# A recurrence and a token mixer on one core: v permuted on TensorE for every unit, uncentred decays, one-piece X sums and another order of steps

## Chip, core and metric

The kernel runs on one core of one Trainium2 chip, in one launch. The metric is device time in microseconds (us). The engines are TensorE (PE, with its weight loads as PEld), VectorE (DVE), ScalarE (ACT), GpSimd (POOL) and SyncE (SP), which issues nearly all DMAs.

## The reference, cut to what matters

Inputs r, k, v, w have shape (4 batches, 8 heads, 768 tokens, 48), u is (8, 48). A recurrence gives x of 384 columns per token, and a mixer over all tokens of a batch follows.

```python
for t in range(S):
    cur = np.einsum('bhd,bhe->bhde', u[None] * kt, vt)
    y[:, :, t] = np.einsum('bhd,bhde->bhe', rt, state + cur)
    state = wt[:, :, :, None] * state + np.einsum('bhd,bhe->bhde', kt, vt)
x = y.transpose(0, 2, 1, 3).reshape(B, S, H * D)
W_tok = scale * (x @ w_q) @ (x @ w_k).T          # per batch, 768 x 768
out = np.maximum(W_tok @ x, 0.0) @ w_out
```

## The kernel before, in words

Each batch's 768 tokens are three **units** of 256 tokens, so there are 12 units, 0 to 11; a unit is two chunks of 128 tokens. `unit(n, batch)` declares the steps of a unit, each with the engines that may do it:

- Loads by SP into rings of four buffers: `wg`, `kg`, `rg`, `vg`. `load` brings rows of two tokens of a head (96 values, 384 bytes), `load_long` rows of four tokens (768 bytes). In the last batch (units 9 to 11) v comes instead as `vw`: four loads for the whole batch, each of runs of one token (48 values, 192 bytes).
- `ln` (ACT) takes the log of the decays into `lw`; `cw` (PE) sums them along the tokens; `ep` and `en` (ACT) are the exponentials of plus and minus those sums. The log is offset by a constant MU, which centres the sums; `gx`, `gv`, `gk`, the scaled mask `US` and the scaled identity `IDU` undo that later.
- `k16`, `r16`, `v16` are casts to bf16. `kT`, `rT` (PE) transpose k and r with the permutation `PM`; `vp` (PE) permutes v's tokens in four products of 64x384, and `VB` copies the result out of PSUM. In the last batch `VB` is cast by POOL straight from `vw`, with no `v16` and no `vp`.
- `ks` copies kT; `qT`, `RT`, `KT` are products of r and k with each other and with the exponentials. `A` (PE) is KT by RT for each head, and `AM` (DVE) multiplies it with the causal mask US. `kb`, `kd` turn KT back; `sn` (PE) and `SB` (DVE) are the running state. `uT` and `UB` transpose u once, and `dps`, `dd`, `Vd` make the bonus of a token's own value.
- `yi` and `ya` (PE) sum state and mask products, and `X` (DVE) adds `Vd`: X = y * gx + Vd, in two instructions of 384 columns.
- `xt`, `XT`, `qk`, `QK` (in the last unit `wq`, `wk` and their copies) make the mixer's queries and keys from X. After a batch's last unit, `T` sums keys by X over the batch and `TS` copies it; then for each unit `mx` (PE), `rl` (relu), `fp` (PE, six products with w_out for a whole step, three for a half one), `os` (copy) and `st` (store). In the first and last unit several steps come in halves.

The order is a table: `ORDER` lists the step numbers, `WAYS` gives the engine (or form) of each step that has a choice, `BANKS` the PSUM bank of each buffer. In `WAYS`, A, D, P are ScalarE, VectorE, GpSimd; E, e, c are forms of products; d is a KT product read from PSUM. Every engine runs its own steps in that order and waits for what each needs. Eighteen products of zeros warm TensorE up at the start, and twelve more (`z`) stand in the table. The functions that the change touches:

Of the kernel before, what the change touches and what calls it, by code (L numbers as in the profile page):

```python
# [32 lines left out]
class Plan:  # L33
# [89 lines left out]
]  # L123
WAYS = (
    "PDDDAPPDDdPADPPDDEEEAAPPAdPAAPEAcEEAAPPAPPADPeDEEDAAAAAAAAPPDPDADPeAcEEDAPPAdPAAPEAEEEDA"
    "PPDPPAAPeAEEAAAAAAAAAAPDPPAAPEDEcEAAPPDPPDAPEAEEEAAPPDPPAAPeDceAAAAADADDPAAPPAPEDcEEDAPP"
    "DPPAPeAcceAAPPDPPPAPPAEEDDAEDADAAADAAAADADDA"
)
BANKS = [
# [13 lines left out]
def kernel(  # L143
# [12 lines left out]
    nc = tc.nc  # L156
# [15 lines left out]
    WHOLE = (B - 1,)  # L172

    SHIFT = 25
    MU = -SHIFT * math.log(2.0) / C
    UNIT = 2.0 ** -SHIFT

# [9 lines left out]
    def const(shape, dtype, name):  # L187
# [15 lines left out]
        QK=(2, QW, BF16), TS=(2, DM, BF16), vw=(2, NCH * DM, F32))  # L203
    if not WHOLE:
        del RINGS["vw"]
# [15 lines left out]
    IDU = const([C, C], BF16, "IDU")  # L221
    Z = const([C, 512], BF16, "Z")
    US = const([C, C], F32, "US")
    CM = const([C, 2 * C], BF16, "CM")
    pos0 = const([C, 1], I32, "pos0")
    pos1 = const([C, 1], I32, "pos1")
    gx = const([C, 1], F32, "gx")
    gv = const([C, 1], F32, "gv")
    gk = const([C, 1], F32, "gk")
# [18 lines left out]
    def setup():  # L248
# [9 lines left out]
        for q in range(4):  # L258
            rows = ds(64 * (q % 2) + 32 * (q // 2), 32)
            nc.gpsimd.iota(pos0[rows, :], pattern=[[0, 1]], base=q, channel_multiplier=4)  # L260
            nc.gpsimd.iota(pos1[rows, :], pattern=[[0, 1]], base=q + 1, channel_multiplier=4)
# [632 lines left out]
```

## Time and profile before

| | |
|---|---|
| median of 3 runs | 101.71 us (101.36 to 102.08) |
| span of the profiled execution, first to last instruction | 99.6 us (the only time given of that execution) |
| busy, share of the span | PE 87%, DVE 85%, ACT 79%, POOL 70% |
| DMA, mean | 24.68 MB in 45141 packets, 248 GB/s |
| granted TensorE clock | full throughout |

Busy times are unions of an engine's instructions; matmuls are pipelined and their ends are modelled, so a busy PE is not PE at its peak. In a timeline row stand start, duration, engine, source line, operation and output <- inputs with their shapes, and in brackets the idle time ahead and what ended it. Instructions of one engine overlap a little, so the distance from one start to the next is what a step costs its queue. A group row has busy time, mean duration of one in ns, and idle time ahead.

### The profile page before, as it was taken

How to read it: one execution, taken by the hardware profiler on the slowest of the kernel's cores; microseconds unless marked ns; L12 is line 12 of the kernel's file. 1: busy time of each engine (PE TensorE's matmuls, PEld its weight loads, DVE VectorE, ACT ScalarE, POOL GpSimd, SP SyncE). 2: the span in 40 equal slices, each digit the busy share in tenths (PEclk: the TensorE clock that was granted, in tenths of full speed). 3: DMA queues.
4: the chain of work that ended last, by engine and by line, in shares of the span. 5: the costliest groups of instructions: out<-in, count | busy, mean ns of one | idle time of the engine just before them, and what ended most of it. 6: DMA issues, size and time to landing. Idle time of an engine off the chain costs nothing.

```text
span 99.6 us, 4492 instructions
## 1 busy us (share of the span) xinstructions
PE 86.6 (87%) x1906; PEld 63.3 (64%) x1911; DVE 84.9 (85%) x154; ACT 79.0 (79%) x135; POOL 69.5 (70%) x82
## 2 busy tenths in 40 slices
PE   5978796879886998999999999889998999999930
PEld 1325473756774767777776777759787687776610
DVE  6284999799979999979999999999999799783740
ACT  6034998799996799899999998999899766666920
POOL 6866354999799895799999989498996392500000
PEclk9999999999999999999999999999999999999999
DMA  1999999799999999999999977998993056030794
GB/s 17 313 327 349 324 337 296 195 295 335 289 314 298 225 311 329 344 321 268 271 330 305 316 114 218 251 156 201 282 417 115 7 210 264 10 158 7 277 367 149
DMA packets 45141, 24.68 MB, mean 248 GB/s; under 512 B 31552, under 2 KB 43968, under 8 KB 45120
## 3 DMA queue, kind: packets, MB, share of 16 engines
q1 hardware_dynamic: 44960, 24.19, 84.0%
q8 instruction: 15, 0.25, 0.9%
q10 hardware_dynamic: 160, 0.20, 0.5%
q14 instruction: 6, 0.05, 0.1%
HBM read 19.66 MB, written 4.72 MB: 245 GB/s over the span
## 4 chain that ended last, share of the span: by engine, by line
PE 37%; DVE 23%; SPq 20%; DMA 7%; issue 7%; ACT 3%; ACTq 0%; DVEq 0%
PE PS L179 37%; SPq L232 9%; SPq L237 8%; DMA vg<-in_v_dram 7%; DVE AM L595 7%; DVE X L710 6%; DVE RT L516 3%; SPq L355 2%; DVE qT L506 2%; DVE ks L333 2%; DVE SB L658 1%; ACT VB L327 1%; SPq L357 1%; ACT MX L339 1%; DVE kd L335 1%
## 5 line engine op out<-in xcount | busy, mean ns | idle before, releaser
L595 DVE TENSOR_TENSOR AM<-PS,US 128x1024 bf16<-128x1024 f32 x24 | 28.8, 1218 | 0.7 <-PE PS L179 0.7
L526 POOL TENSOR_TENSOR KT<-ks,en 128x1024 bf16<-128x1024 bf16 (+1 forms) x10 | 19.7, 1965 | 4.7 <-DVE ks L333 3.3
L575 POOL TENSOR_TENSOR Vd<-VB,dd 128x768 bf16<-128x768 bf16 (+1 forms) x14 | 18.1, 1293 | 4.5 <-ACT dd L327 3.4
L454 ACT ACTIVATE en<-PS 128x1024 bf16<-128x1024 f32 (+1 forms) x14 | 12.5, 907 | 3.0 <-PE PS L179 2.9
L179 PEld LDWEIGHTS <-KT 48*128 48x128 bf16 (+1 forms) x312 | 9.7, 94 | 6.6 <-issue 4.5
L447 ACT ACTIVATE ep<-PS 128x512 bf16<-128x512 f32 (+1 forms) x28 | 13.7, 555 | 0.1
L179 PE MATMUL PS<-wo,MX 128*128 128x384 bf16 x72 | 13.5, 327 | 0.0
L710 DVE SCALAR_TENSOR_TENSOR X<-PS,gx,Vd 128x384 bf16<-128x384 f32 x22 | 12.5, 609 | 0.7 <-PE PS L179 0.6
L407 ACT ACTIVATE lw<-wg 128x768 bf16<-128x768 f32 x12 | 10.3, 857 | 2.9 <-DMA wg<-in_w_dram 2.9
L179 PE MATMUL PS<-RT,KT 48*128 48x128 bf16 x192 | 9.7, 218 | 1.2 <-ACT VB L327 0.4
L327 ACT COPY os<-PS 128x768 f32<-128x768 f32 (+1 forms) x11 | 7.9, 714 | 3.5 <-PE PS L179 3.5
L418 POOL CAST k<-kg 128x768 bf16<-128x768 f32 x10 | 8.3, 827 | 2.5 <-DMA kg<-in_k_dram 2.5
L179 PE MATMUL PS<-Z 128*128 128x512 bf16 x25 | 8.4, 461 | 1.4 <-DVE Z L250 1.2
L418 POOL CAST r<-rg 128x768 bf16<-128x768 f32 x10 | 8.2, 825 | 1.6 <-DMA rg<-in_r_dram 1.6
L179 PEld LDWEIGHTS <-MX 128*128 128x128 bf16 x72 | 6.5, 97 | 3.6 <-DVE MX L341 0.2
L516 DVE TENSOR_TENSOR RT<-PS,ep 128x1024 bf16<-128x1024 bf16 (+1 forms) x14 | 8.4, 605 | 0.0
L179 PE MATMUL PS<-VB,AM 128*128 128x48 bf16 x192 | 8.0, 184 | 0.4 <-issue 0.4
L506 DVE TENSOR_TENSOR qT<-PS,ks 128x1024 bf16<-128x1024 bf16 x12 | 8.2, 684 | 0.1
L339 ACT ACTIVATE MX<-PS 128x768 bf16<-128x768 f32 (+1 forms) x12 | 8.0, 682 | 0.4
L179 PE MATMUL PS<-CM,lw 64*128 64x128 bf16 x192 | 7.4, 217 | 0.5 <-DVE AM L595 0.3
L327 ACT CAST VB<-PS 128x768 bf16<-128x768 f32 x8 | 6.4, 804 | 1.1 <-PE PS L179 0.6
L179 PEld LDWEIGHTS <-AM 128*128 128x128 bf16 x192 | 6.3, 96 | 1.6 <-issue 0.7
(90 smaller groups left out, 191.9 us busy)
## 6 DMA issues: line engine op xcount, KB each, us to landing
kg<-in_k_dram SPq DMA_DIRECT2D x12, 384.0 KB, 6.4
wg<-in_w_dram SPq DMA_DIRECT2D x12, 384.0 KB, 5.0
rg<-in_r_dram SPq DMA_DIRECT2D x12, 384.0 KB, 5.8
vg<-in_v_dram SPq DMA_DIRECT2D x9, 384.0 KB, 6.3
out_dram<-os SPq DMA_DIRECT2D x9, 384.0 KB, 2.5
vw<-in_v_dram SPq DMA_DIRECT2D x4, 288.0 KB, 6.7
out_dram<-os SPq DMA_DIRECT2D x5, 192.0 KB, 2.4
wof<-in_moe_w_out_dram SPq DMA_DIRECT2D x1, 576.0 KB, 6.2
```

Source lines behind the costliest of these rows:

```text
L179: return nc.tensor.matmul(o, l, rr, start=start, stop=stop, skip_group_check=True, is_transpose=trans)
L327: nc.scalar.copy(o, i)
L407: nc.scalar.activation(view(lw.tile, 0, [[64, H], [512, 2], [1, D]]), view(g["wg"].tile, 0, [[D2, H], [D, 2], [1, D]]), ACT.Ln, bias=0.0, ...
L418: op(view(o.tile, 0, [[64, NP], [256, 4], [1, D]]), view(g[src].tile, 0, [[2 * D2, NP], [D, 4], [1, D]]))
L447: nc.scalar.activation(view(ep.tile, cs[0] * NP * EW + off, [[EW, NP * len(cs)], [step, 2], [1, 32]]), view(at(cw), cs[0] * 512 + j * 64, ...
L454: nc.scalar.activation(en.tile[:, ds(cs[0] * 512, w_)], at(cw)[:, ds(cs[0] * 512, w_)], ACT.Exp, bias=0.0, scale=-1.0)
L506: lambda e: nc.vector.tensor_tensor(plain(qT.tile), turned(512), plain(ks.tile), ALU.mult),
L516: nc.vector.tensor_tensor(plain(RT.tile, cs, 32), turned(512, cs, True), plain(ep.tile, cs, EW // 4), ALU.mult)
L526: x.tensor_tensor(KT.tile[:, cols], ks.tile[:, cols], en.tile[:, cols], ALU.mult)
L575: (nc.vector if e == "D" else nc.gpsimd).tensor_tensor(Vd.tile[:, cols], VB.tile[:, cols], view(dd.tile, cs[0] * H, [[1, len(cs) * H], [0, ...
L595: AMs[c] = add(("AM", n, c), "D", lambda e, c=c, A=A: nc.vector.tensor_tensor(view(AM[c].tile, 0, [[C, 8], [1, C]]), view(at(A), 0, [[C, 8 ...
L710: nc.vector.scalar_tensor_tensor(view(X.tile, 2 * i * DM + hh * D, [[D2, H], [1, D]]), view(at(y), hh * 512, [[D, H], [1, D]]), gx, view(V ...
```

## The change

1. Units 1 to 11 load v with `load_long`, in rows of four tokens. `v16` holds it in another layout, and `vp` has 16 products (8 groups of 32 output rows and 192 columns for each half of the heads) instead of four. `vw` and `load_whole` are gone, so units 9 to 11 have `v16`, `vp` and `VB` like the others. Unit 0 keeps its four products.
2. The decays are not centred: `ln` has scale 1, and the position fills, `gx`, `gv`, `gk`, `IDU` and the scaling of US are gone. `kd` is a plain copy, and `sn` uses the plain identity.
3. X is one sum of y and Vd over 768 columns, and in the last unit two of 384.
4. `ORDER`, `WAYS` and `BANKS` are new tables throughout.

```diff
-    WHOLE = (B - 1,)
-    SHIFT = 25
-    MU = -SHIFT * math.log(2.0) / C
-    UNIT = 2.0 ** -SHIFT
...
-        nc.scalar.activation(gx, pos0, ACT.Exp, bias=0.0, scale=MU)
-        nc.scalar.activation(gv, pos1, ACT.Exp, bias=0.0, scale=-MU)
...
-        nc.vector.tensor_scalar_mul(IDU, ID16, UNIT)
-        nc.vector.tensor_scalar_mul(gk, gv, UNIT)
-        nc.vector.tensor_scalar_mul(US, US, gv)
...
-        for name, ap in (("wg", w), ("kg", k), ("rg", r)) + (() if whole else (("vg", v),)):
-            f = load_long if name in ("kg", "rg") and long else load
+        for name, ap in (("wg", w), ("kg", k), ("rg", r), ("vg", v)):
+            f = load_long if name != "wg" and long else load
...
-                                 bias=0.0, scale=math.exp(-MU))
+                                 bias=0.0, scale=1.0)
...
-        if whole:
-            VBs = add(("VB", n), "PAD", lambda e: copy(
-                e, view(VB.tile, 0, [[D, H], [DM, 2], [1, D]]),
-                view(batch["vw"].tile, 2 * i * D, [[NCH * D, H], [D, 2], [1, D]])),
-                batch["vwL"], VB, [batch["vw"]], cols=2 * DM)
+        v16, vp = ring("v16"), wide()
+        if long:
+            v16v, vgv = [[D, NP], [NP * D, 4], [1, D]], [[2 * D2, NP], [D, 4], [1, D]]
         else:
...
+            if long:
+                for hq in range(2):
+                    for s in range(4):
+                        for c in range(2):
+                            mm(x[ds((s % 2) * 64 + (s // 2) * 32, 32),
+                                 ds(c * 512 + hq * NP * D, NP * D)],
+                               PM[ds(c * 64, 64), ds(c * 64 + hq * 32, 32)],
+                               v16.tile[ds(c * 64, 64), ds(s * NP * D, NP * D)])
+                return
...
-                copy(e, view(kd.tile, 64 + cs[0] * 1024, [[256, n4], [128, 2], [1, D]]), x, gk)
+                copy(e, view(kd.tile, 64 + cs[0] * 1024, [[256, n4], [128, 2], [1, D]]), x)
...
-                    mm(x[rows, ds(0, NP * D)], IDU[:, rows], old.tile, start=True, stop=False)
+                    mm(x[rows, ds(0, NP * D)], ID16[:, rows], old.tile, start=True, stop=False)
...
-                for hh in range(2) if not end else ():
-                    nc.vector.scalar_tensor_tensor(
-                        view(X.tile, 2 * i * DM + hh * D, [[D2, H], [1, D]]),
-                        view(at(y), hh * 512, [[D, H], [1, D]]), gx,
-                        view(Vd.tile, hh * D, [[D2, H], [1, D]]), ALU.mult, ALU.add)
+                if not end:
+                    nc.vector.tensor_tensor(
+                        view(X.tile, 2 * i * DM, [[D, 2], [D2, H], [1, D]]),
+                        view(at(y), 0, [[512, 2], [D, H], [1, D]]),
+                        view(Vd.tile, 0, [[D, 2], [D2, H], [1, D]]), ALU.add)
...
 ORDER = [
-    0, 3, 13, 2, 21, 22, 23, 15, 16, 17, 1, 24, 25, 26, 27, 28, 29, 76, 77, 78, 31, 73, 74, 75,
+    0, 1, 2, 3, 4, 15, 16, 17, 30, 21, 22, 23, 24, 25, 26, 33, 34, 36, 27, 28, 29, 31, 14, 18,
```

What the tables move is seen in the engines' queues, of which three places follow. A name like `ks_0_95` is buffer 0 of the ring `ks`; `PS_62` is PSUM.

**VectorE at the start**, from the cast of u to the first mask product of unit 0; ahead of it stand the setup's fills, before also the scaling of US and the pads of both `kd` buffers, after the pads of one. Before:

```order
L333 CAST uC_134<-uR_133 8x128
L333 COPY ks_0_95<-PS_62 128x1024
L526 TENSOR_TENSOR KT_0_101<-ks_0_95,en_0_93 128x512
L521 TENSOR_TENSOR KT_0_101<-PS_62,en_0_93 128x512
L516 TENSOR_TENSOR RT_0_99<-PS_62,ep_0_91 128x512
L506 TENSOR_TENSOR qT_0_97<-PS_62,ks_0_95 128x1024
L335 TENSOR_SCALAR kd_0_83<-PS_62,gk_152 128x8x48
L516 TENSOR_TENSOR RT_0_99<-PS_62,ep_0_91 128x512
L335 TENSOR_SCALAR kd_0_83<-PS_62,gk_152 128x8x48
L595 TENSOR_TENSOR AM0_0_111<-PS_62,US_146 128x1024
```

After:

```order
L300 CAST uC_132<-uR_131 8x128
L382 CAST r16_0_87<-rg_0_67 128x8x2x48
L300 COPY UB_133<-PS_62 128x8
L300 COPY ks_0_95<-PS_62 128x1024
L467 TENSOR_TENSOR qT_0_97<-PS_62,ks_0_95 128x1024
L482 TENSOR_TENSOR KT_0_101<-PS_62,en_0_93 128x512
L477 TENSOR_TENSOR RT_0_99<-PS_62,ep_0_91 128x512
L482 TENSOR_TENSOR KT_0_101<-PS_62,en_0_93 128x512
L477 TENSOR_TENSOR RT_0_99<-PS_62,ep_0_91 128x512
L562 TENSOR_TENSOR AM0_0_111<-PS_62,US_143 128x1024
```

The cast of r and the copy of UB have come in ahead of ks, and the two kd copies have gone to ScalarE. On TensorE, `uT`, `kT` and `cw` of unit 0 stood in that sequence, and now `cw`, `kT`, `rT`, `uT`; on SP, `wg` is now loaded ahead of `kg`.

**VectorE from ks of unit 10 to a mask product of unit 9.** Before:

```order
L333 COPY ks_0_95<-PS_62 128x1024
L710 SCALAR_TENSOR_TENSOR X_0_125<-PS_62,gx_150,Vd_0_109 128x8x48 x2
L506 TENSOR_TENSOR qT_0_97<-PS_62,ks_0_95 128x1024
L516 TENSOR_TENSOR RT_0_99<-PS_62,ep_0_91 128x1024
L335 TENSOR_SCALAR kd_1_84<-PS_62,gk_152 128x16x48
L595 TENSOR_TENSOR AM0_1_112<-PS_62,US_146 128x1024
L658 TENSOR_TENSOR SB_3_118<-PS_62,ep_1_92 128x192
L595 TENSOR_TENSOR AM1_1_114<-PS_62,US_146 128x1024
```

After:

```order
L300 COPY ks_0_95<-PS_62 128x1024
L300 COPY XT_1_120<-PS_62 128x768
L467 TENSOR_TENSOR qT_0_97<-PS_62,ks_0_95 128x1024
L677 TENSOR_TENSOR X_0_125<-PS_62,Vd_0_109 128x2x8x48
L477 TENSOR_TENSOR RT_0_99<-PS_62,ep_0_91 128x1024
L300 COPY kd_1_84<-PS_62 128x16x48
L300 COPY XT_0_119<-PS_62 128x768
L562 TENSOR_TENSOR AM0_1_112<-PS_62,US_143 128x1024
L625 TENSOR_TENSOR SB_3_118<-PS_62,ep_1_92 128x192
L300 CAST QK_0_127<-PS_62 128x384
L562 TENSOR_TENSOR AM1_1_114<-PS_62,US_143 128x1024
```

Two XT copies and a QK copy, which were ScalarE's, stand here now; X is one instruction.

**GpSimd in units 9 to 11.** Before, from KT of unit 9 on:

```order
L526 TENSOR_TENSOR KT_1_102<-ks_1_96,en_1_94 128x1024
L526 TENSOR_TENSOR KT_0_101<-ks_0_95,en_0_93 128x1024
L333 CAST VB_1_106<-vw_0_131 128x8x2x48
L333 CAST VB_0_105<-vw_0_131 128x8x2x48
L575 TENSOR_TENSOR Vd_1_110<-VB_1_106,dd_1_108 128x768
L418 CAST k16_1_90<-kg_3_74 128x4x4x48
```

After, from KT of unit 10 on:

```order
L487 TENSOR_TENSOR KT_0_101<-ks_0_95,en_0_93 128x1024
L300 CAST v16_0_103<-vg_2_77 128x4x4x48
L542 TENSOR_TENSOR Vd_1_110<-VB_1_106,dd_1_108 128x768
L300 CAST v16_1_104<-vg_3_78 128x4x4x48
L379 CAST k16_1_90<-kg_3_74 128x4x4x48
```

Where GpSimd wrote VB of units 9 and 10 itself, it now casts v of units 10 and 11 into v16, and TensorE (`vp`) and ScalarE (`VB`) finish them; on TensorE both those `vp` stand ahead of `ya` of unit 9. On SP the last loads were `vw` (three), `kg`, `wg`, `rg`, then all stores; now they are `vg` (unit 9), `wg`, the store of unit 1, `vg` (10), `vg` (11), `kg`, `rg`, then the other stores.

More of the change, by code (lines that the diff above doesn't have):

```diff
@@ L202 @@
         SB=(4, NP * D, BF16), XT=(2, 2 * DM, BF16), MX=(4, 2 * DM, BF16), X=(2, NCH * DM, BF16),
-        QK=(2, QW, BF16), TS=(2, DM, BF16), vw=(2, NCH * DM, F32))
-    if not WHOLE:
-        del RINGS["vw"]
+        QK=(2, QW, BF16), TS=(2, DM, BF16))
     tiles = {k: [const([C, w_], ty, f"{k}_{i}") for i in range(n)]
@@ L322, in at, with copy @@
         return x if dtype == F32 else x.bitcast(dtype)
-    def copy(e, o, i, by=None):
+    def copy(e, o, i):
         if e == "A":
-            if by is None:
-                nc.scalar.copy(o, i)
-            else:
-                nc.scalar.activation(o, i, ACT.Copy, bias=0.0, scale=by)
-        else:
-            x = nc.gpsimd if e == "P" else nc.vector
-            if by is None:
-                x.tensor_copy(o, i)
-            else:
-                x.tensor_scalar_mul(o, i, by)
+            nc.scalar.copy(o, i)
+        else:
+            (nc.gpsimd if e == "P" else nc.vector).tensor_copy(o, i)
     def relu(e, o, i):
@@ L388, in unit @@
         fine = each if split else both
-        whole, long = b in WHOLE, n in LONG
+        long = n in LONG
         g = {}
-        for name, ap in (("wg", w), ("kg", k), ("rg", r)) + (() if whole else (("vg", v),)):
-            f = load_long if name in ("kg", "rg") and long else load
+        for name, ap in (("wg", w), ("kg", k), ("rg", r), ("vg", v)):
+            f = load_long if name != "wg" and long else load
             g[name] = ring(name)
@@ L398, in unit @@
                 bonus(g["wgL"])
-        if whole and i == 0:
-            batch["vw"] = ring("vw")
-            batch["vwL"] = [dma(("vw", n, q), lambda e, q=q, x=batch["vw"].tile:
-                                load_whole(b, q, x), buf=batch["vw"]) for q in range(4)]
         lw = ring("lw")
@@ L535, in unit @@
         VB = ring("VB")
-        if whole:
-            VBs = add(("VB", n), "PAD", lambda e: copy(
-                e, view(VB.tile, 0, [[D, H], [DM, 2], [1, D]]),
-                view(batch["vw"].tile, 2 * i * D, [[NCH * D, H], [D, 2], [1, D]])),
-                batch["vwL"], VB, [batch["vw"]], cols=2 * DM)
-        else:
-            v16, vp = ring("v16"), wide()
-            v16s = add(("v16", n), "PAD", lambda e: copy(
-                e, view(v16.tile, 0, [[D, H], [DM, 2], [1, D]]),
-                view(g["vg"].tile, 0, [[D2, H], [D, 2], [1, D]])), [g["vgL"]], v16, [g["vg"]])
-            def f_vp(e):
-                x = at(vp)
-                for j in range(2):
-                    for c in range(2):
-                        rows = ds(c * 64, 64)
-                        mm(x[ds(j * 64, 64), ds(c * 512, DM)], PM[rows, rows],
-                           v16.tile[rows, ds(j * DM, DM)])
-            vps = add(("vp", n), "E", f_vp, [v16s], vp, [v16], mode=3)
-            VBs = add(("VB", n), "AD", lambda e: copy(
-                e, view(VB.tile, 0, [[DM, 2], [1, DM]]), view(at(vp), 0, [[512, 2], [1, DM]])),
-                [vps], VB, [vp], cols=2 * DM)
+        v16, vp = ring("v16"), wide()
@@ new lines, in unit, with f_vp @@
+        if long:
+            v16v, vgv = [[D, NP], [NP * D, 4], [1, D]], [[2 * D2, NP], [D, 4], [1, D]]
+        else:
+            v16v, vgv = [[D, H], [DM, 2], [1, D]], [[D2, H], [D, 2], [1, D]]
+        v16s = add(("v16", n), "PAD", lambda e: copy(
+            e, view(v16.tile, 0, v16v), view(g["vg"].tile, 0, vgv)), [g["vgL"]], v16, [g["vg"]])
+        def f_vp(e):
+            x = at(vp)
+            if long:
[7 more added lines that the diff above has]
+                return
+            for j in range(2):
+                for c in range(2):
+                    rows = ds(c * 64, 64)
+                    mm(x[ds(j * 64, 64), ds(c * 512, DM)], PM[rows, rows],
+                       v16.tile[rows, ds(j * DM, DM)])
@@ L559, in unit @@
+        vps = add(("vp", n), "E", f_vp, [v16s], vp, [v16], mode=4 if long else 3)
+        VBs = add(("VB", n), "AD", lambda e: copy(
+            e, view(VB.tile, 0, [[DM, 2], [1, DM]]), view(at(vp), 0, [[512, 2], [1, DM]])),
+            [vps], VB, [vp], cols=2 * DM)
         dps, dd = bank(), ring("dd")
```

29 lines of the change are left out of this document (7 added, 22 removed), and 90 rows, old and new, of tables (BANKS, ORDER).

## Prediction

> **What bounds the kernel now.** I read the engine totals first, then the table by stretch, then the chain that ended last, and last each engine's timeline.
>
> ```profile
> PE 86.6 (87%) x1906; PEld 63.3 (64%) x1911; DVE 84.9 (85%) x154; ACT 79.0 (79%) x135; POOL 69.5 (70%) x82
> ...
> 40.00:50.00 10.00, 9.64 (x234) 7.44 (x232) 9.45 (x16) 9.62 (x16) 9.55 (x8) 1.00 1.07 301
> 60.00:70.00 10.00, 9.42 (x276) 7.47 (x274) 10.00 (x17) 9.64 (x16) 8.24 (x7) 1.00 1.00 214
> 80.00:90.00 10.00, 9.84 (x189) 7.48 (x190) 8.84 (x17) 6.07 (x13) 4.14 (x4) 1.00 0.41 160
> ```
>
> In the rows by stretch the pairs of figures are PE, PEld, DVE, ACT, POOL, then the granted clock, the DMA share and GB/s. From 40 to 70 us VectorE (DVE) has no slack worth the name, ScalarE (ACT) little, and the DMA engines are full. From 80 us on only TensorE is full. The chain names the same change of hands.
>
> ```profile
> 65.98 1.14 DVE AM L595
> ...
> 67.17 9.67 PE PS L179 x260
> ...
> 85.56 10.02 PE PS L179 x107
> ```
>
> So the time is: VectorE's queue up to its last mask product `AM` (85.57 us), and then some 14 us of small steps that no queue shortens much: the last X, its products, the last batch's token products and output projections, the store. I therefore sum what the change does to VectorE's queue up to that product, then ask what the others allow.
>
> **Durations on VectorE**, as distance from one start to the next, since neighbours overlap by some 0.08 us:
>
> ```profile
> 28.62 1.31 DVE L333 CAST v<-vg 128x768 bf16<-128x768 f32 x1 [0.73 <-DMA vg<-in_v_dram]
> 29.85 0.68 DVE L506 TENSOR_TENSOR qT<-PS,ks 128x1024 bf16<-128x1024 bf16 x1
> ...
> 31.05 1.13 DVE L710 SCALAR_TENSOR_TENSOR X<-PS,gx,Vd 128x384 bf16<-128x384 f32 x2
> 32.10 0.67 DVE L521 TENSOR_TENSOR KT<-PS,en 128x1024 bf16<-128x1024 bf16 x1
> 32.70 0.16 DVE L333 COPY dd<-PS 128x16 f32<-128x16 f32 x1
> 32.85 0.56 DVE L333 COPY XT<-PS 128x768 bf16<-128x768 bf16 x1
> 33.38 1.23 DVE L595 TENSOR_TENSOR AM<-PS,US 128x1024 bf16<-128x1024 f32 x1
> 34.52 0.35 DVE L658 TENSOR_TENSOR SB<-PS,ep 128x192 bf16<-128x192 f32 x1
> ...
> 54.19 0.61 DVE L335 TENSOR_SCALAR kd<-PS,gk 128x768 bf16<-128x768 bf16 x1
> 54.71 1.22 DVE L595 TENSOR_TENSOR AM<-PS,US 128x1024 bf16<-128x1024 f32 x1
> ...
> 56.11 0.95 DVE L333 CAST VB<-PS 128x768 bf16<-128x768 f32 x1
> 56.97 0.68 DVE L333 COPY ks<-PS 128x1024 bf16<-128x1024 bf16 x1
> ```
>
> *X.* A unit's X is now two instructions, 32.10-31.05 = 1.05 us. It becomes one sum of 768 columns, which the trace does not show. From below, AM does 1024 fp32 columns from PSUM in 34.52-33.38 = 1.14 us, so 768 of them 0.855; from above, nothing is gained (1.05). The VB copy of 768 fp32 columns took 56.97-56.11 = 0.86, and I take 0.87: 0.18 us for each of 11 units, **-2.0 us**; the ends are 0 and -2.2.
>
> *Steps that the new order hands out differently*, counted up to the last AM. Off VectorE: the cast of v of unit 3 (29.85-28.62 = 1.23), the VB copy of unit 7 (0.86), two `dd` copies (0.15 each), and of `kd` six calls become three. The six were two of 768 columns (0.52) and four of 384 (some 0.33 by 54.71-54.19 less the 0.2 us that half the columns save), 2.35 in all; three of 768 make 1.55. Together -3.2 us. Onto VectorE: three XT copies (33.38-32.85 = 0.53), two QK copies of 384 fp32 columns (about half of VB's, 0.45), one ks (its 0.68 less the overlap, 0.6), and `KT`: two whole units of 32.70-32.10 = 0.60 both now and after, two half calls now and four after, 0.6 us more for the two. Together +3.7 us. The sum is **+0.5 us**, and with X **-1.5 us** on VectorE.
>
> *Start.* What precedes the first AM moves most.
>
> ```profile
> 1.23 5.73 PE L179 MATMUL PS<-Z 128*128 128x512 bf16 x18 [1.23 <-DVE Z L250]
> 7.64 0.17 PE L179 MATMUL PS<-ID,uC 8*128 8x8 bf16 x1 [0.68 <-DVE uC L333]
> ...
> 6.69 0.83 POOL L421 CAST r<-rg 128x768 bf16<-128x768 f32 x1 [0.73 <-DMA rg<-in_r_dram]
> ...
> 8.52 0.69 DVE L333 COPY ks<-PS 128x1024 bf16<-128x1024 bf16 x1 [0.94 <-PE PS L179]
> ...
> 12.62 1.22 DVE L595 TENSOR_TENSOR AM<-PS,US 128x1024 bf16<-128x1024 f32 x1
> ```
>
> The warm-up products leave TensorE at 1.23+5.73 = 6.96 us, but it then waits until 7.64 for `uC`, which VectorE casts behind the scaling of US and two sets of pads; the transpose of k and the decay sums stand behind that. In the changed order the decay sums come first, then kT and rT, and only then uC's transpose, so TensorE can begin at about 7.0, and ScalarE's exponentials follow. Against that, VectorE now casts r of unit 0 (1.23 us as for v, from 6.69, when rg has landed) and waits for uC's transpose behind rT, so ks starts at about 8.6, as now. From there to AM it has qT, two KT and two RT, 0.6 + 0.6 + 4 x 0.33 = 2.5 us, where 12.62-8.52 = 4.1 us passed: AM at about 11.2, 1.4 us sooner. Some 0.65 of it are the two `kd` calls counted above. **-0.7 us**, between 0 and -1.4. The scaling of US, the scaled identity, GpSimd's eight position fills and two exponentials, which the change drops, all lie ahead of that first ks, so they have no other price.
>
> *End.* After the product T of the last unit TensorE now has five whole projections of six products; the changed order has four (one whole, six halves), and the fifth stands where the last XT is copied.
>
> ```profile
> 83.96 1.14 PE L179 MATMUL PS<-wo,MX 128*128 128x384 bf16 x6
> ```
>
> TensorE waits little there now, so a projection mostly moves: I give it **-0.3 us**, between 0 and -1.1, its own length.
>
> *TensorE.* v goes through 16 products of 32x192 output where there were 4 of 64x384, and the three units of the last batch, which had none, get them too.
>
> ```profile
> 37.05 0.36 PE L179 MATMUL PS<-v,PM 64*64 64x384 bf16 x4
> 37.34 0.40 PE L179 MATMUL PS<-RT,KT 48*128 48x128 bf16 x8
> ...
> 50.15 0.40 PE L179 MATMUL PS<-PM,r 64*128 64x64 bf16 x16
> 50.48 0.35 PE L179 MATMUL PS<-UB,qT 128*128 128x2 bf16 x8
> ...
> L179 PE MATMUL PS<-v,PM 64*64 64x384 bf16 x36 | 3.2, 346 | 0.7 <-DVE RT L516 0.7
> ```
>
> Four products of 346 ns each fit into 0.36 us, so those on different quarters of the array run side by side; the step occupies 37.34-37.05 = 0.29 us. The new ones use eighths, so two rounds of eight of half the length. Below: the same 0.29; above, if sixteen cost as sixteen transposes do plus the columns, 50.48-50.15 = 0.33 for 64 columns, three times that for 192, 1.0 us. Nearest is the row of the same data, and I take 0.40: 8 x 0.11 + 3 x 0.40 = 2.1 us more. Beside VectorE's queue most of it is hidden; between 67 and 77 us, where the chain runs through TensorE, 1.2 us come together, and I charge **+0.8 us** in all.
>
> The Trainium skill speaks against these sixteen: "TensorE: Matmul & The Clock Gate", The mechanism, has weight loads overlap running products only where their row group differs, and eight of the sixteen share each row group. By that rule the sum would be the last rival's below. The trace does not agree: products three and four of the step at 37.05 share row groups with the first two, and all four are done within 0.36 us.
>
> *ScalarE* gets four more VB copies in all and gives up XT, QK and ks, and `kd` loses its scale, 901 ns against 800 for an XT of the same size:
>
> ```profile
> L329 ACT ACTIVATE kd<-PS,gk 128x768 bf16<-128x768 bf16 x5 | 4.5, 901 | 1.0 <-PE PS L179 0.9
> ...
> L327 ACT COPY XT<-PS 128x768 bf16<-128x768 bf16 x7 | 5.6, 800 | 1.1 <-PE PS L179 1.1
> ```
>
> Up to mx of unit 3 (some 66 us) it has one VB more, and one XT, one ks and one QK less; by columns at 0.80 for 768 that is +0.80 -0.80 -1.07 -0.40. Of `kd`, four whole calls and a half one (4.05 us) become three whole and five halves (4.40 at the lower price). That makes -1.1 us, less the fixed cost of four more calls, three of them small `dd` copies, which no row here separates: I take **-0.6 us**. It does not bind harder than VectorE, nor much less.
>
> *DMA.* v of the last batch came in runs of 192 bytes; in the stretch that holds three of its four loads the engines were as full as before, 1.00 against 1.07, and moved 214 GB/s instead of 301. With 0.88 MB of v in those 10 us, the other 1.26 MB at 281 (301/1.07) need 4.5 us, so v took 5.5 us against 3.1 at that rate: 2.4 for three loads, **3.2 us** for all four. That, and a little for the other units' longer runs, shortens the loads, which are beside VectorE's work; I count nothing for it. Uncentred decays change a constant, and cost nothing.
>
> **Sum:** -1.5 -0.7 -0.3 +0.8 = -1.7 us on the profiled execution's 99.6 us of span, 97.9. The runs' median, 101.71, lies 2.1 us over that span (no other time of that execution is given); with the same 2.1 the forecast is **100.0 us**, 1.7% faster. Its own range is 98.3 to 101.5: down by the lower ends of start (0.7 more), end (0.8) and X (0.2), up by a start of nothing (0.7) and TensorE's 2.1 us uncovered instead of 0.8 (1.3), which would make 102.0 and hardly come together.
>
> **Rivals.** *The saving lands beside the path.* The one sum of X costs what the two cost (then +2.0), or ScalarE, busy for 9.62 and 9.64 of 10 us at 40 and 60, takes only its own 0.6 us off: 99.6 - 0.6 - 0.3 (end) + 0.8 = 99.5, so 101.6. For it: in the rows at 40 and 60 three engines stand at 9.4 of 10 or more. Against: ScalarE also gains at the start. Chance 0.24.
>
> *A wait for v in the last batch (slower).* The products of v for units 10 and 11 both stand ahead of ya of unit 9 on TensorE, and unit 11's needs a cast that GpSimd (POOL) does behind Vd of unit 9.
>
> ```profile
> 64.34 1.48 POOL L575 TENSOR_TENSOR Vd<-VB,dd 128x768 bf16<-128x768 bf16 x1 [1.45 <-ACT dd L327]
> ...
> 72.61 1.48 POOL L575 TENSOR_TENSOR Vd<-VB,dd 128x768 bf16<-128x768 bf16 x1
> 74.04 0.83 POOL L418 CAST k<-kg 128x768 bf16<-128x768 f32 x1
> ...
> 74.42 0.36 PE L179 MATMUL PS<-VB,AM 128*128 128x48 bf16 x8
> ...
> 78.81 1.16 POOL L526 TENSOR_TENSOR KT<-ks,en 128x512 bf16<-128x512 bf16 x1 [2.41 <-DVE ks L333]
> ```
>
> At today's pace that cast would stand at 74.04 and end at 74.87, the product and its 0.40 at 75.3, while ya of unit 9 ran at 74.42: 0.9 us late, with everything behind it on TensorE. It decides from the point at which GpSimd is later than now relative to TensorE; if Vd waits as it does at 64.34 and 78.81 (1.45 to 2.41), the loss is 2.4 to 3.3 us on top of the sum: 102.4 to 103.3. On SyncE's queue the store of unit 1 now stands ahead of the last two loads of v: its 384 KB take some 1.3 us of full engines (at 301 GB/s), which the shorter loads above give back. Against it: GpSimd is busy 70% of the span and loses two KT. Chance 0.15, two thirds of it over 1% slower.
>
> *The loads were the brake.* The DMA share is full to 70 us, and if compute follows it, the 3.2 us come on top of the start and the end: 99.6 - 3.2 - 1.0 = 95.4, so 97.5. Against: VectorE is busy all of 60 to 70 us while the loads run; its wait for one of them at 28.62 is 0.73 us. Chance 0.08.
>
> *The sixteen products do not overlap.* Each row group's eight in series, 8 x (103 ns load + 80 ns for 192 columns) = 1.46 us a unit, 8 x 1.17 + 3 x 1.46 = 13.7 us on TensorE, of which its idle 13 of 100 hide a part: some 110. Both figures are rows:
>
> ```profile
> L179 PEld LDWEIGHTS <-PM 64*64 64x64 bf16 x36 | 1.1, 103 | 1.8 <-issue 1.1 <-ACT VB L327 0.2
> 35.12 0.25 PE L179 MATMUL PS<-SB,IDU 128*128 128x192 bf16 x1
> 35.20 0.36 PE L179 MATMUL PS<-VB,kd 128*128 128x48 bf16 x8
> ```
>
> Chance 0.03, for the row at 37.05.
>
> **Chances.** The forecast's case holds 0.50. About 1% is what a measurement of this kernel can tell from no change: 100.7 to 102.7. The forecast's own range lies to three quarters or more below 100.7, 0.44 faster and 0.06 the same; with the loads' 0.08 that is 0.52 faster. The first rival (0.24) and a third of the second (0.05) make 0.35 the same with that 0.06; the rest, 0.13, is slower. To hold 8 in 10 the range reaches from the loads' case to the late v: 97.6 to 102.9.
>
> **What would show it.** X as one instruction of 0.95 us or less in the group table; v's sixteen within 0.5 us on the timeline; the first AM near 11.2 us and the last ending near 84.0; VectorE without a new wait over 1 us; some 8,700 DMA packets fewer (four loads of 1536 runs and eight of 1024 become eleven of 512). The prediction is wrong if TensorE waits for v before ya of unit 9, if X shows 1.1 us or more, or if the waits on VectorE grow by 2 us or more, since then the order and not the work decides.

## The result, and the profile after

The changed kernel takes 106.5 us in the median (105.16 to 108.25) against 101.71 us: 1.050 times the time of the kernel before, 95% interval 1.044 to 1.056. Forecast were 100.0 us, between 97.6 and 102.9. The profiled execution, the fastest of the five runs, took 105.16 us, with a span of 103.5. Medians below include disturbed runs; the ratios to the kernel before, which lead wherever both stand, leave them out.

The page after, engine totals, packets, and the row of the queue that carries instructions:

```profile
PE 87.3 (84%) x2082; PEld 63.5 (61%) x2087; DVE 82.5 (80%) x140; ACT 78.7 (76%) x136; POOL 67.3 (65%) x74
...
DMA packets 36422, 24.70 MB, mean 239 GB/s; under 512 B 17200, under 2 KB 35248, under 8 KB 36400
...
q8 instruction: 16, 0.26, 1.0%
```

VectorE has 2.4 us less work (84.9 before), yet every engine's share fell: all wait more. The table by stretch, columns as in the prediction, first of after, then one row of before:

```profile
40.00:50.00 10.00, 9.44 (x243) 7.09 (x245) 9.31 (x16) 9.77 (x16) 8.43 (x7) 1.00 1.02 308
57.00:60.00 3.00, 1.29 (x61) 1.12 (x56) 1.42 (x2) 2.30 (x4) 1.68 (x3) 1.00 1.11 328
60.00:70.00 10.00, 8.74 (x241) 6.86 (x242) 9.71 (x14) 8.07 (x16) 8.45 (x7) 1.00 0.92 301
80.00:90.00 10.00, 9.84 (x224) 7.08 (x219) 9.30 (x16) 7.16 (x15) 2.26 (x3) 1.00 0.11 41
```

```profile
57.00:60.00 3.00, 2.76 (x70) 2.34 (x67) 3.00 (x7) 3.00 (x7) 2.70 (x3) 1.00 0.70 117
```

Between 57 and 60 us VectorE works 1.42 of 3 us, where before it worked all 3, and TensorE, which nothing should hold, 1.29. The timelines show how, and the two other new waits above 1 us. First VectorE, from the first mask product on:

```profile
11.79 1.22 DVE L562 TENSOR_TENSOR AM<-PS,US 128x1024 bf16<-128x1024 f32 x1
...
29.25 0.69 DVE L467 TENSOR_TENSOR qT<-PS,ks 128x1024 bf16<-128x1024 bf16 x1 [1.13 <-ACT ks L298]
29.86 0.95 DVE L677 TENSOR_TENSOR X<-PS,Vd 128x768 bf16<-128x768 f32 x1
30.73 1.22 DVE L562 TENSOR_TENSOR AM<-PS,US 128x1024 bf16<-128x1024 f32 x1
...
35.68 0.69 DVE L482 TENSOR_TENSOR KT<-PS,en 128x1024 bf16<-128x1024 bf16 x1 [1.08 <-ACT ks L298]
...
60.02 0.69 DVE L300 COPY ks<-PS 128x1024 bf16<-128x1024 bf16 x1 [1.55 <-PE PS L174]
...
87.85 1.22 DVE L562 TENSOR_TENSOR AM<-PS,US 128x1024 bf16<-128x1024 f32 x1
```

The last mask product ends at 87.85+1.22 = 89.07 us, 3.5 us later than before, although the first started 0.83 us sooner. Between the two, VectorE's idle time (the stretch less its busy time) grew from 72.95-69.91 = 3.04 to 77.28-69.95 = 7.33 us; 1.13, 1.08 and 1.55 are most of the 4.3. Behind the first two stands ScalarE, behind the third TensorE:

```profile
28.21 1.01 ACT L298 COPY ks<-PS 128x1024 bf16<-128x1024 bf16 x1 [1.99 <-DVE RT L477]
...
34.63 1.01 ACT L298 COPY ks<-PS 128x1024 bf16<-128x1024 bf16 x1 [0.99 <-DVE RT L477]
```

```profile
54.80 0.36 PE L174 MATMUL PS<-v,PM 64*32 64x192 bf16 x16
55.09 0.31 PE L174 MATMUL PS<-VB,kd 128*64 128x48 bf16 x8
...
57.39 0.34 PE L174 MATMUL PS<-PM,k 64*128 64x64 bf16 x11
59.43 0.24 PE L174 MATMUL PS<-PM,k 64*128 64x64 bf16 x5 [1.71 <-issue]
```

So there are two mechanisms to test. **The bank's turns:** `ks` on ScalarE and `RT` on VectorE read the same PSUM buffer `kr`. In the new table RT of units 3 and 4 stands ahead of ks, so ScalarE, idle for 1.99 us, begins only as RT ends, and VectorE then waits for ks. **The supply of instructions:** TensorE stops after 11 of 16 transposes for which everything is there ("issue": no semaphore holds it).

The second has a clock of its own in the trace. Counting TensorE's recorded instructions (products and weight loads) from the start, the four longest such stops of its products lie at 447, 2493, 2749 and 3004: 447 plus 8, 9 and 10 times 256, less the two or three records that are missing. The packets of q8 are 16 KB each, one to 256 instructions (15 before with 3825 records, 16 after with 4179). Worked out from the trace, in us, for four block ends of after and of runs told below:

```
kernel, instructions    block before   packet    end of block   TensorE
from the start          ended          starts    reached        goes on
after, 2493             53.76          56.80     57.53          59.43
after, 3517             74.82          74.95     78.88          79.00
e4,     958             22.76          26.19     26.78          28.78
e13,   2497             54.27          56.26     58.12          58.64
```

The packet sets out after the block before has ended: in the change 0.1 to 0.5 us after it when the DMA engines have little to do (behind 74 us), 1.4 to 3.0 us while loads fill them. Loads are not the whole of it: at 69.90 us in the change, and at three block ends of e13 between 58 and 70 us, the packet took 1.0 to 1.4 us to set out with the engines idle (a share of 0.04 or less), and why is not shown. In the profiles of this case, some forty block ends were reached less than 2.3 us after their packet's start; TensorE went on 2.3 to 2.8 us after that start, twice later (2.88 and 3.06). A block that TensorE runs through in less than the sum of the two delays therefore ends in a stop. The Trainium skill ("Runtime: NRT & Kernel Launch", Instruction fetch mechanics) has blocks of 16 KiB and 256 instructions that the sequencer fetches while it runs the block before, and calls the cost mostly hidden. The trace agrees on the size and not on the cost: 1.9 us at 57.53.

### The profile page after: what moved, and what is told of

Its sections match the earlier page's. It is cut to its first block, busy times and chain, and to the rows that moved or that the text cites. A ratio compares the mean times of both kernels' runs of the same rounds, so it can differ in the third digit from the quotient of the medians.

```text
span 103.5 us, 4814 instructions
## 1 busy us (share of the span) xinstructions
PE 87.3 (84%) x2082; PEld 63.5 (61%) x2087; DVE 82.5 (80%) x140; ACT 78.7 (76%) x136; POOL 67.3 (65%) x74
## 5 line engine op out<-in xcount | busy, mean ns | idle before, releaser
L487 POOL TENSOR_TENSOR KT<-ks,en 128x1024 bf16<-128x1024 bf16 x8 | 17.1, 2132 | 4.4 <-DVE ks L300 2.9
L298 ACT COPY os<-PS 128x768 f32<-128x768 f32 (+1 forms) x12 | 8.8, 729 | 4.6 <-PE PS L174 4.5
L300 POOL CAST v<-vg 128x768 bf16<-128x768 f32 x12 | 9.9, 827 | 1.9 <-DMA vg<-in_v_dram 1.9
L677 DVE TENSOR_TENSOR X<-PS,Vd 128x768 bf16<-128x768 f32 x11 | 10.5, 951 | 0.5 <-POOL Vd L542 0.4
L174 PE MATMUL PS<-Z 128*128 128x512 bf16 x25 | 9.1, 503 | 1.5 <-DVE Z L231 1.2
L304 ACT ACTIVATE MX<-PS 128x768 bf16<-128x768 f32 (+1 forms) x13 | 9.1, 719 | 1.6 <-PE PS L174 1.2
L298 ACT CAST VB<-PS 128x768 bf16<-128x768 f32 x12 | 9.8, 814 | 0.2
```

The costliest lines, as they stand in the source:

```text
L174: return nc.tensor.matmul(o, l, rr, start=start, stop=stop, skip_group_check=True, is_transpose=trans)
L298: nc.scalar.copy(o, i)
L300: (nc.gpsimd if e == "P" else nc.vector).tensor_copy(o, i)
L304: nc.scalar.activation(o, i, ACT.Relu)
L487: x.tensor_tensor(KT.tile[:, cols], ks.tile[:, cols], en.tile[:, cols], ALU.mult)
L677: nc.vector.tensor_tensor(view(X.tile, 2 * i * DM, [[D, 2], [D2, H], [1, D]]), view(at(y), 0, [[512, 2], [D, H], [1, D]]), view(Vd.tile, 0 ...
```

## The experiments

**Parts of the change, one by one.** *e1* is the kernel before, its tables and loads, with the new arithmetic alone:

```diff
-                                 bias=0.0, scale=math.exp(-MU))
+                                 bias=0.0, scale=1.0)
...
-                    nc.vector.scalar_tensor_tensor(
...
+                    nc.vector.tensor_tensor(
...
```

> The kernel before, its order, engines, banks and loads of v untouched; only X is one sum of 768 columns and the decays are not centred. If the order made the change slow, the arithmetic alone is a gain: 11 X of 0.80 to 0.87 us for 1.05 take 2.0 to 2.6 us off VectorE, of which some reaches the end: 99 to 101 us, with VectorE's idle time between the first and the last AM at 3 to 4 us, as before (2.99). If TensorE's instruction supply made it slow, the same, since this kernel has the 3824 TensorE rows of before. If the one sum or the uncentred decays were themselves at fault, it is slower than 101.7 us.

Ratio 0.994, interval 0.989 to 0.999 (median 102.19 us, 100.15 to 103.82): the arithmetic is a gain of 0.6%, against the 0.7 to 2.7 us expected. *e5* adds four-token rows and sixteen products for v in units 1 to 8:

```diff
-            f = load_long if name in ("kg", "rg") and long else load
+            f = load_long if name != "wg" and long else load
...
+                if long:
+                    for hq in range(2):
+                        for s in range(4):
+                            for c in range(2):
...
```

> As the run with the old order and the new sums, and v of units 1 to 8 in four-token rows through sixteen products; the last batch's v still comes whole, without products, so that the old order can stand. If the order made the change slow: within 0.7 us of that run, 99 to 101.5 us, each step of sixteen products within 0.4 us. If TensorE's instruction supply did it: 96 more products (192 instructions) add unwaited gaps on TensorE of over 1 us, and 1 to 2 us to the time. If the sixteen products themselves are dear: 8 steps of 1 us and more, 103 us or more.

Median 104.48 us (103.55 to 106.0), 3.4 us over e1 by the lowest runs, though the old order stands. Its profile has stops of 1.4 us at 1214 instructions and 1.8 us at 2749. *e4* is the reverse, the changed kernel with two-token rows and four products:

```diff
-            f = load_long if name != "wg" and long else load
+            f = load_long if name in ("kg", "rg") and long else load
...
-            if long:
-                for hq in range(2):
...
```

> The changed kernel with its order, engines and banks, but v in two-token rows through four products in units 1 to 11: 132 products (264 instructions) fewer on TensorE. If the order made the change slow, it stays: 105 to 107 us, with the waits of VectorE for the ks of units 3 and 4 (about 1.1 us each) where they were. If TensorE's instruction supply did it, the gap of 1.7 us inside the transposes of unit 8 is gone and the time falls to 102 to 104 us. If loads count, the 11 x 512 more packets of v add up to 1 us.

Ratio 1.010, interval 1.005 to 1.016 (median 103.5 us). So by ratios the arithmetic is worth -0.6%, the order +1.6%, the sixteen products +4.0%, together the change's +5.0%. (The order's part here includes the last batch's v, which e4 loads and permutes like the other units' and e1 does not.) TensorE has 132 products fewer, and the stop is gone from unit 8; in this profile it stands at 958 instructions, in another step:

```profile
26.37 0.62 PE L174 MATMUL PS<-CM,lw 64*128 64x128 bf16 x16
28.78 0.27 PE L174 MATMUL PS<-SB,RT 48*128 48x48 bf16 x8 [1.78 <-issue]
```

```profile
20.00:29.70 9.70, 7.47 (x215) 6.20 (x210) 7.76 (x12) 7.85 (x14) 8.58 (x9) 1.00 1.09 305
29.70:33.10 3.40, 3.40 (x38) 2.59 (x38) 2.68 (x4) 2.36 (x4) 2.71 (x4) 0.50 0.94 247
```

Behind it comes a second price: for 3.4 us TensorE is granted half its clock (0.50) and does 38 products, where 75 would fit at the pace of the row above.

*e6* moves two steps of VectorE away from the waits for ks (steps by name and unit, in the table's order):

```diff
-RT.3 ks.3 qT.3
-X.2
+RT.3 ks.3
+X.2 qT.3
...
-RT.4 ks.4 KT.4
+RT.4 KT.4 ks.4
```

> The changed kernel with two steps moved on VectorE: qT of unit 3 behind X of unit 2, and KT of unit 4 ahead of ks of unit 4 (a step of ScalarE). If the waits of VectorE for ks in units 3 and 4 (1.13 and 1.08 us) make up the loss, they are gone and 1 to 2 us with them: 104 to 105.5 us. If the loss comes later, from TensorE's gap in unit 8 or from the order behind it, the time stays at 105.5 to 107 us although these two waits are gone: the gain is taken back by a wait for TensorE or ScalarE before the last AM.

107.3 us (105.33 to 108.12). Its profile has stops of 1.7 and 1.3 us at 2493 and 2749 instructions; whether moving the waits helped can't be read from it.

**Which property of the sixteen products.** *e7* keeps e4's loads and layout, but cuts each of its four products into four:

```diff
+            n4 = 4 if long else 1
+            for q in range(n4):
...
+                           v16.tile[rows, ds(j * DM + q * DM // n4, DM // n4)])
```

> The changed kernel's order with v in two-token rows, as in the run with four products, but each of the four products of units 1 to 11 cut into four of 96 columns: TensorE has the 264 more instructions again, v's loads, casts and layout stay those of four products. If the supply of instructions to TensorE costs the time, it is slow as the changed kernel, 105 to 107 us, with unwaited gaps on TensorE of over 1 us where a multiple of 256 instructions is passed. If the longer runs or the cast of v cost it, it stays with the run with four products: 102.5 to 104.5 us.

Ratio 1.027, interval 1.016 to 1.038 (median 105.58 us), 1.7% over e4, and the stop is back in unit 8, at 2497:

```profile
57.62 0.34 PE L174 MATMUL PS<-PM,k 64*128 64x64 bf16 x11
60.18 0.24 PE L174 MATMUL PS<-PM,k 64*128 64x64 bf16 x5 [2.23 <-issue]
```

Neither v's rows nor its cast differ from e4: the number of instructions alone brings the stop back. It does not account for the whole cost: 1.7% of the 4.0% between e4 and the change. e7's four runs spread from 103.6 to 108.7 us, and whether the rest belongs to the longer rows, or only to where the stops happen to fall, is not shown. *e10* was to shift the block ends by 36 instructions:

```diff
-        for _ in range(18):
-            mm(PS[:, ds(0, 512)], Z[:, ds(0, C)], Z)
+        for _ in range(36):
+            mm(PS[:, ds(0, 256)], Z[:, ds(0, C)], Z[:, ds(0, 256)])
```

> The changed kernel with the 18 warm-up products of 512 columns as 36 of 256 columns: the same work at the start, 36 TensorE instructions more. If the gaps lie at block ends of 256 instructions, they stay at the same counts from the start (447, 2493, 2749 and so on) and so come 36 instructions earlier in the program: the gap of 1.9 us is no longer in the transposes of k of unit 8 but ahead of them. If a step of the program stalls (the transposes of unit 8), the gap stays in it. The time: 104.5 to 107 us by both.

Ratio 1.040, interval 1.031 to 1.048; but the profiled execution took 145.6 us and is no guide to where the others stopped, so the run leaves its question open. Two other profiles answer it: at 2749 instructions the change stops inside the transposes of r (0.48 us from start to start) and e5 inside the products of SB by RT (1.79). The count is the same and the step another.

**Fewer loads.** *e8* and *e9* leave out r of units 4 to 11, with sixteen and with four products:

```diff
+   skip=(name == "rg" and n > 3): skip or f(b, i, x, ap)
```

> The changed kernel without the loads of r of units 4 to 11 (those units work on r of units 0 to 3). Instructions and order stay. If TensorE stalls because the 16-KB packets of its instructions queue behind loads (they start 1.4 to 3.0 us after the last block's end while the DMA engines are full, 0.1 to 0.5 us once they are not), they now start earlier, the gaps of 1.90, 0.48 and 0.45 us go, and the time falls by 2 to 3 us: 102.5 to 104.5 us. If the order's waits on VectorE are the cost, less traffic takes off 1 us at most: 105 us or more.

> The changed kernel's order with four products for v, without the loads of r of units 4 to 11: the partner of the run before it. If the sixteen products cost time through the supply of instructions, the 3 us between four and sixteen shrink to 1 us or less when the loads are fewer: 101.5 to 103.5 us here. If the sixteen cost time on TensorE by themselves, the 3 us stay: this one some 3 us below its partner.

106.18 us (104.01 to 106.45) and 102.67 (ratio 1.011, 1.001 to 1.020): by the medians the gap between them stays, 3.5 us (1.8 by the lowest runs), which spoke against the theory. But the loads that were left only moved up; up to 57 us the DMA engines were full, the packet for the block at 2497 started 4.2 us after the block before, and the stop in unit 8 grew to 2.79 us. *e13* and *e14* therefore leave out k, r and v of those units (`name != "wg"` in the same line):

> The changed kernel without the loads of k, r and v of units 4 to 11 (these units work on data of units 0 to 3); only w is still loaded. Leaving out r alone had let the loads end some ten us sooner, but up to 57 us the DMA engines were as full as before. Now they should be nearly idle from about 35 us on. If TensorE stalls because its instruction packets start late beside loads, from then on each starts within 0.6 us of the last block's end, TensorE has no gap at a block end behind 35 us, and the time falls to 101.5 to 104 us. If the order's waits or the sixteen products are the cost, it stays at 105 us or more.

> The same loads left out, with four products for v instead of sixteen. If the sixteen cost only through late instructions, this one and its partner lie within 1 us (3 us apart with all loads). If they cost TensorE's time by themselves, some 3 us stay between them.

103.9 us (ratio 1.024, 1.011 to 1.036) and 101.95 (1.005, 1.002 to 1.009). By the ratios the sixteen products gain 2.5% by it and four 0.5%, as the theory of late packets has it; but 1.8% (2 us) stay between them, which neither expectation allowed for. Nor did every packet set out within 0.6 us: the one for the block at 2497 took 2.0 us (DMA share 0.55 from 54.27 to 56.27). Where the 2 us are lost, the rows say: X of unit 1 and the first X of unit 11, of e13 and then of e14.

```profile
26.81 0.95 DVE L678 TENSOR_TENSOR X<-PS,Vd 128x768 bf16<-128x768 f32 x1
...
87.76 0.56 DVE L683 TENSOR_TENSOR X<-PS,Vd 128x384 bf16<-128x384 f32 x1
```

```profile
25.16 0.94 DVE L666 TENSOR_TENSOR X<-PS,Vd 128x768 bf16<-128x768 f32 x1
...
86.19 0.56 DVE L671 TENSOR_TENSOR X<-PS,Vd 128x384 bf16<-128x384 f32 x1
```

From there on both need the same, 60.95 and 61.03 us, though in e13 each unit has sixteen products instead of four, and the cast that goes with them: by themselves these cost nothing. The 1.65 us between them are lost ahead of it, while the DMA engines were still full. TensorE's rows and clock of e13, and the same stretch of e14:

```profile
15.85 0.60 PE L174 MATMUL PS<-CM,lw 64*128 64x128 bf16 x15
17.21 0.21 PE L174 MATMUL PS<-CM,lw 64*128 64x128 bf16 x1 [0.76 <-issue]
...
57.98 0.34 PE L174 MATMUL PS<-PM,k 64*128 64x64 bf16 x11
58.64 0.24 PE L174 MATMUL PS<-PM,k 64*128 64x64 bf16 x5 [0.33 <-issue]
```

```profile
19.50:23.00 3.50, 3.50 (x67) 2.30 (x65) 2.70 (x6) 2.60 (x5) 3.50 (x3) 0.53 0.99 276
```

```profile
19.50:23.00 3.50, 3.33 (x80) 2.66 (x76) 3.50 (x7) 3.46 (x8) 3.50 (x3) 1.00 0.98 274
```

A stop at the block end at 449 instructions, then a stretch at half clock. The stop in unit 8 has shrunk from 1.71 to 0.33 us.

**Fewer instructions.** *e11* (changed kernel) and *e12* (e1) do kb and xt in whole forms:

```diff
+                if s["ways"] == "eE":
+                    s["way"] = "E"
```

> The changed kernel with every kb and xt that the table does in halves (16 or 12 small transposes) done whole (8 or 6 large ones): 136 TensorE instructions fewer, on TensorE itself no faster (0.6 us for 8 large, 0.4 for 16 small). If the supply of instructions costs the time, 0.5 to 2 us less than the changed kernel: 104 to 106 us. If TensorE's work itself does, it is 0.5 to 2 us slower.

> The kernel before with the one sum for X and decays not centred, and the kb and xt in halves done whole: 80 TensorE instructions fewer than before. If the supply of instructions matters, 0 to 1 us below the run with the old order and the new sums, so 99.5 to 101.5 us, and so faster than both kernels. If TensorE's work does, 0.5 to 1 us above it.

106.46 us (ratio 1.051, 1.040 to 1.062) and 101.98 (1.001, 0.996 to 1.006): no gain; e12 lies 0.7% above e1, as the theory of TensorE's own work had it. In e11 the transposes of k of unit 8 run through, the block end at 2497 now stands behind them and costs 0.24 us from start to start, and a stop of 0.9 us has come at 2753: what 136 instructions fewer saved, if anything, the longer products and other stops took.

**The order's own share.** With few loads the times scatter less (ten runs of e14 lie within 0.7 us, ten of e4 within 3.8). *e15* is e1 with k and r of units 4 to 11 and v of units 4 to 8 left out, the same line as above:

> The old order with the one sum and decays not centred, without the loads of k and r of units 4 to 11 and of v of units 4 to 8 (those units work on data of units 0 to 3; v of the last batch is still loaded whole, in four loads). If the new order costs time by its own waits, this one is 1 to 2 us below the new order with four products and few loads (101.95 us): 100 to 101 us. If the order cost only through TensorE's late instructions, the two are within 0.5 us.

100.13 us (ratio 0.987, 0.973 to 1.000) against 101.95: the new order's own cost is some 1.8 us, with a wide interval, and again with the last batch's v in it. *e16* is e14 with e6's two moves:

> The new order with four products and few loads (k, r and v of units 4 to 11 left out) and with the two steps moved (qT of unit 3 behind X of unit 2, KT of unit 4 ahead of ks of unit 4). If VectorE's waits for ks in units 3 and 4 (1.13 and 1.08 us) make up the order's share, they are gone and the time falls by 1 to 2 us, to 100 to 101 us. If another wait takes their place, it stays within 0.5 us of 101.95 us.

104.22 us (1.030, 1.017 to 1.042), 2.3 us slower. Part of that is a stop of 1.09 us at 961 instructions, which the profile of e14 has not. And the wait was not out, only passed on; ScalarE, TensorE and VectorE in turn:

```profile
35.44 1.01 ACT L295 COPY ks<-PS 128x1024 bf16<-128x1024 bf16 x1 [1.65 <-DVE KT L480]
...
36.58 0.76 PE L171 MATMUL PS<-VB,AM 128*128 128x48 bf16 x15 [1.42 <-ACT dd L295]
...
38.84 0.36 DVE L611 TENSOR_TENSOR SB<-PS,ep 128x192 bf16<-128x192 f32 x1 [1.66 <-PE PS L171]
```

With KT ahead too, ks waited for two reads of VectorE; `dd` and `VB` of unit 3 are queued behind ks on ScalarE, TensorE waited for them and then had 3.4 us of half clock. *e17* and *e18* go at the turns themselves, on e14: ks of units 3 and 4 on VectorE, and on ScalarE but first.

```diff
+                if s["key"] in (("ks", 3), ("ks", 4)):
+                    s["way"] = "D"
```

```diff
-rT.3 KT.3
-RT.3 ks.3 qT.3
+rT.3 ks.3 KT.3
+RT.3 qT.3
...
-rT.4 RT.4 ks.4 KT.4
+rT.4 ks.4 RT.4 KT.4
```

> The new order with four products and few loads (k, r and v of units 4 to 11 left out), and ks of units 3 and 4 done by VectorE in their old places instead of by ScalarE. If the turns of two engines on one bank are the order's share, the waits of 1.13 and 1.08 us go, VectorE gets 1.2 us of work for them, ScalarE is free for what stood behind ks, and the time falls by 0.8 to 1.8 us from 101.95: 100.1 to 101.2 us. If the order loses elsewhere, it stays at 101.7 to 102.5 us.

> The same kernel with ks of units 3 and 4 on ScalarE, but placed right behind rT, ahead of VectorE's KT and RT of that unit. If the turns cost, ScalarE takes the bank while it stood idle (2.2 and 1.0 us), VectorE waits 0.7 us or less for it, and the time falls by 1 to 2 us: 100 to 101 us. If the wait only changes its place, VectorE waits 1 us ahead of KT or RT, and the time stays within 0.5 us of 101.95 us.

100.78 us (0.999, 0.994 to 1.004) and 100.82 (0.994, 0.990 to 0.998): by the medians both ways gain 1.1 us of the 1.8, by the ratios 0.6 and 1.1%. VectorE's rows of e17, where nothing waits now, and of e18, where KT waits 0.96 us and qT not at all:

```profile
27.10 0.68 DVE L302 COPY ks<-PS 128x1024 bf16<-128x1024 bf16 x1
27.82 0.69 DVE L470 TENSOR_TENSOR qT<-PS,ks 128x1024 bf16<-128x1024 bf16 x1
```

```profile
27.07 0.69 DVE L480 TENSOR_TENSOR KT<-PS,en 128x1024 bf16<-128x1024 bf16 x1 [0.96 <-ACT ks L295]
...
28.28 0.68 DVE L465 TENSOR_TENSOR qT<-PS,ks 128x1024 bf16<-128x1024 bf16 x1
```

The other 0.7 us of the order were not traced.

**Mended, with all loads.** *e19* is the changed kernel with e18's order, *e20* the same with four products:

> The changed kernel, whole, with all loads and sixteen products, and ks of units 3 and 4 on ScalarE placed right behind rT, ahead of VectorE's KT and RT. If the turns on the bank and the late instruction packets add up, 1 us less than the changed kernel: 104.5 to 106 us, TensorE's gaps at block ends staying. If late packets take the gain back, 106 us or more.

> The same with four products for v, all loads: 1 us less than the new order with four products (103.5 us), so 101.8 to 103 us, level with the kernel before, if the two costs add up; 103.3 us or more if late packets take the gain back.

e19 takes 106.69 us (ratio 1.048, 1.041 to 1.054), no gain; e20 101.33 (0.994, 0.989 to 0.999), 0.6% below the kernel before, level with e1, and by the ratios 5.4% below the change, with TensorE's clock full throughout its profile. In e19 the gain met new stops, the longest of them with a stretch of half clock behind it:

```profile
36.14 0.39 PE L171 MATMUL PS<-RT,KT 48*128 48x128 bf16 x7
38.46 0.21 PE L171 MATMUL PS<-RT,KT 48*128 48x128 bf16 x1 [1.94 <-issue]
```

Its waits for ks were down to 0.65 and 0.34 us, but it stopped at 1473, 2497 and 2753 instructions for 2.15, 1.36 and 1.30 us from start to start. Between e19 and e20 stand only the two kinds of v rows and 264 instructions: 5.4%.

## Why the prediction was wrong, step by step

*TensorE, +0.8 us: the step that failed.* It priced sixteen products by the time they occupy the array, 0.40 us a unit. That was even too dear: from 54.80 to 55.09 they take 0.29, as four did. What the runs show in its place is the supply of their instructions, 24 more in each of units 1 to 8 and 32 in the last three, beside loads: stops at block ends and the half clock that often follows. Sixteen against four cost 1.8% with few loads and 4.0 to 5.4% with all; e7 ties 1.7% to the number of instructions alone, and what makes up the rest stays open. No row of the trace before was read for this, though it had such stops: 0.7 us inside the transposes of k near 77 us, 0.4 to 0.6 at 28, 39 and 46 us, small enough to pass as noise.

*Steps handed out differently, +0.5 us.* As work it holds: up to the last mask product the distances on the timeline add up to 0.4 us more for these steps and 1.9 less for X. The step counted ks by engine and duration, and not that a ks on ScalarE takes turns with RT and KT of its own unit on VectorE. In the old table ks stood ahead of RT; in the new one it stands behind it in units 3 and 4, some 1.1 us of the order's 1.8.

*X, -2.0 us*: the size was right, 30.73-29.86 = 0.87 us as taken, but e1 gives only 0.6% for it and the decays together: most of it lies beside the path, as the first rival had it for its own reasons. *Start, -0.7 us*: the first mask product came at 11.79, not 11.2, so 0.83 us sooner instead of 1.4; without the `kd` calls counted elsewhere 0.2 instead of 0.7. *End, -0.3 us*: from the last mask product to the end of the span it is 103.5-89.07 = 14.4 us for 14.0, no gain. *DMA, nothing*: packets fell by 8,719 as forecast (some 8,700); but loads are not without effect, since instruction packets wait beside them.

*Rivals.* The late v of the last batch did not come: from 65 us to the last mask product VectorE waits 0.30 us at most, and TensorE has no wait above 0.15 us ahead of v's products. The sixteen products did overlap; that rival had the culprit and the wrong mechanism. The bound set for being wrong, waits on VectorE grown by 2 us, was met with 4.3, but its conclusion "then the order decides" covers the smaller part.

## What to carry to other kernels

Price an added product also by its instructions: where an engine runs 256 of them in less time than a 16-KB instruction packet needs beside the loads (here 1.4 to 3 us to set out, 4.2 in e8, and 2.3 to 2.8 more), it stops, and gaps marked "issue" at equal counts of instructions show it. When a table reorders reads of one PSUM buffer by two engines, look which reads first: the late reader holds up its own queue and whatever waits for it. To judge an order, measure it once with the loads thinned out, so that the supply of instructions doesn't hide it.

## What the runs showed of the hardware

Not expected were the stops themselves, and that packets of the instruction queue wait beside loads: in the change 1.4 to 3.0 us while the DMA share is near 1 and 0.1 to 0.5 us behind 74 us, though 1.0 to 1.4 us at four block ends with the engines idle. Nor was TensorE's half clock in so full a kernel: stretches of 3.4 us at 0.50 followed eight of its twelve gaps above 1.3 us in these profiles (e4's for one), but not the one in the change's own. Seven more such stretches (e13's at 19.7 us, three near 13 us, one of them of 6.8 us) followed no gap that long, so what sets the clock back is not shown. Two engines' reads of one PSUM buffer go one after the other here, held apart by a semaphore: in the change ks begins at 28.21, after RT, which starts at 27.44 and takes 0.68. The Trainium skill ("PSUM — Partial Sum Buffer", PSUM bank collisions raise a hardware error) gives the reason for such turns: two engines at one bank at once are an error, not a wait. No run here shows that error.
